# Long convolution, block 0: transform matmuls placed between products, transfers and small products moved, sums in another order

## The chip, the cores and the metric

One Trainium2 chip, one core. The metric is the device time of one execution in microseconds (us). The engines are PE (matmuls; PEld is its weight load), DVE (vector), ACT (scalar, activations), POOL (GpSimd) and SP, which here only issues DMAs. Each engine works through its own queue in order. DMAs issued by SP travel on queue q1, DMAs issued by POOL on q0; the same 16 DMA engines serve both.

## The reference, cut to what matters

```python
x = A_u                                     # 1 x 2048 x 576
sa, ca, ga, sb, cb, gb = (silu(c) @ w_mod).reshape(1, 6, 1, 576)   # in order
h = layernorm(x) * (1 + ca) + sa
K = 2 * real(sum_n C[d,n] dt[d] exp(A[d,n] dt[d] l))               # 576 x 2048, N = 128
y = irfft(rfft(h, 4096) * rfft(K, 4096))[:2048] + h * D_skip       # a long convolution
x = x + ga * y
h = layernorm(x) * (1 + cb) + sb
out = x + gb * (relu(h @ w1) @ w2)          # 576 -> 4608 -> 576
```

All in float32. Large matmuls are done with values split in a high and a low part of the type fp32r, so that one product takes several matmuls.

## The kernel before, in words

The 2048 positions are worked in four blocks of 512. The convolution is done block by block with transforms of 1024 points in four parts (`transform`, `butterfly1`, `butterfly2`), and the channels of a block in two halves of 288 (p = 0 and 1). Block 0's convolution, `conv0`, stands alone at the start of the program; those of blocks 1 to 3 are generators that are woven into the feed-forward (`ffn`) of the block before. `KGen` makes the kernel K of the convolution: 576 channels in six groups of 96. For a group, powers W1 (built by `doubling`) and W2 are multiplied on PE in `products`: 192 small matmuls. `first` is a generator that `conv0` calls step by step: group 4's doubling and products, group 5's doubling, group 5's products. `rest`, at the start of the feed-forward, makes the rest of K from W1, W2 and Z, which were stored to DRAM (W1d, W2d, Zd) and are loaded again.

The names that matter below:

- early: both tables of the forward transform (fcu, fck), loaded early into a buffer that frees later. fcU, fcK: the same tables in their lasting place. gc: the table of the inverse. fcKn, gcn: negated parts of these.
- ZU, ZK: transforms of h and of K for the first half; U0, K0, Y0, V0: their spectra, the product, and the inverse's first step. Z1, WK, U1, K1, Y1, V1: the same for the second half. `transform1` makes WK by two matmuls for each part, so that no butterfly's first step is needed.
- kd, kt: K's rows, stored to DRAM (`store`) and loaded in another layout (`load_kt`). `src_K` adds the skip weight dsk to kt's first row.
- Ud, Rd: spectra of halves, stored by POOL (`save`).
- sb, cb, gb: products of the conditioning vector with 576x576 pieces of w_mod (`mod_late`), through one buffer wm, one after the other: load on POOL's queue, 25 matmuls, ACT copies, two transposes.
- `back`: the inverse's matmuls ps_i, DVE's addition to x2 (the residual stream) and its statistics st. `norm2`: square roots on ACT, h2, transposes ps_t, and xh, xl, xs for the feed-forward.
- r1, r2 (both r in the profile): pieces of w1 and w2 from DRAM, two buffers each; `split1` and `split2` make the high part w on ACT and the low part on DVE, and the low part is stored (L1d, L2d). hps: the first matmul of the feed-forward; hh, hl: its split result, hh by ACT, hl by DVE, in two PSUM buffers; acc: the second matmul.

The order on each engine is set in three ways. In `conv0` most DVE operations and SP DMAs go through `kept` while `self.pinned` is true, which ties each to the one before it on its engine; what isn't tied is put in order by a scheduler at build time. SP's DMAs use eight semaphores in turn, so a DMA waits until the one eight places ahead has landed.

Of the kernel before, what the change touches and what calls it, by code (L numbers as in the profile page):

```python
# [18 lines left out]
P = 128  # L19
# [27 lines left out]
class KGen:  # L47
# [165 lines left out]
    def doubling(self, g):  # L213
# [4 lines left out]
        for i, m in enumerate((1, 2, 4, 8)):  # L218
            X, out = W1[:, :, 0:m].rearrange(flat), W1[:, :, m : 2 * m]
            zr, zi = (  # L220
                Z[:, r, i].rearrange("p (u c) -> p u c", u=2).unsqueeze(2).broadcast_to([P, 2, 2 * m, H])
                for r in range(2)
            )
            for u in (slice(0, 1), slice(1, 2)) if m > 2 else (slice(0, 2),):
                n = u.stop - u.start
                shape = dict(u=n, a=m, r=2)
                if m == 8:
                    t = self.pt.tile([P, 16 * H], F32, tag="T0", bufs=2, name="T0")
                    T = self.pt.tile([P, 16 * H], F32, tag="T1", bufs=2, name="T1")
                else:  # L230
                    t = self.pt.tile([P, 8 * H], F32, tag="t", bufs=2, name="t")[:, : 2 * n * m * H]
                    T = self.ps.tile([P, 512], F32, tag="T", name="T")[:, : 2 * n * m * H]
                t, T = (x.rearrange("p (u a r c) -> p u a r c", **shape) for x in (t, T))
                v(t.rearrange(flat), X[:, u], zr[:, u], op=ALU.mult)
                v(T.rearrange(flat), X[:, u], zi[:, u], op=ALU.mult)
                add = p if m == 8 else v
                add(out[:, u, :, 0], t[:, :, :, 0], T[:, :, :, 1], op=ALU.subtract)
                add(out[:, u, :, 1], t[:, :, :, 1], T[:, :, :, 0], op=ALU.add)

    def products(self, ps, W1, W2, u):  # L240

        for q in range(12):
            for dd in range(4):
                ch = dd * 12 + q
                for r in range(2):
                    self.nc.tensor.matmul(  # L246
                        ps[32 * dd : 32 * dd + 32, 12 * u + q, :],
                        W2[:, r, :, ch],
                        W1[:, u, :, r, ch],
                        start=(r == 0),  # L250
                        stop=(r == 1),
                    )

    def first(self, setup, mod, norm):
# [52 lines left out]

        def multiply(g):
            kps[g] = self.bank(f"kps_{g}")[:, :384].rearrange("p (q a) -> p q a", a=16)
            for u in range(2):  # L310
                self.products(kps[g], self.W1[g], W2s[g][u], u)

# [33 lines left out]
        double(4)  # L346
        multiply(4)
        yield
# [117 lines left out]
class Body:  # L466
# [108 lines left out]
    def mod_weights(self, w, col, eng):  # L575
        v = self.I["w_mod"]
        eng.dma_start(out=w[:, 0:4], in_=v[0:512, col].rearrange("(k p) c -> p k c", p=P))
        eng.dma_start(out=w[:64, 4], in_=v[512:576, col])

    def mod_lhs(self, cb):  # L580
# [6 lines left out]

    def mod_late(self):

# [4 lines left out]
        for i, nm in ((3, "sb"), (4, "cb"), (5, "gb")):  # L594
            w = cv.tile([P, 5, D], F32, tag="wm", bufs=1, name=f"wm_{nm}")
            self.mod_weights(w, slice(i * D, (i + 1) * D), nc.gpsimd)
            yield
# [118 lines left out]

    def transform(self, src, fc, Z):

        nc = self.nc
        for n2 in (0, 2, 1, 3):  # L720
            for c in range(2):
                ps = self.cps.tile([P, 512], F32, tag="cps", bufs=self.nps, name="ps_f")
                o = ps[:, :PC].rearrange("p (a b) -> p a b", a=4)
                nc.tensor.matmul(o, fc[:, n2, c, :], src(n2), start=True, stop=True)  # L724
                nc.scalar.activation(Z[:, n2, c], ps[:, :PC], AF.Copy)  # L725
# [214 lines left out]
    def norm2(self, s, x2, xp, st=None):  # L940
# [15 lines left out]
        for n2 in range(4):  # L956
            if s == 0 and n2 % 2 == 0:
                nc.vector.tensor_scalar(
                    h2[n2][:, :D], x2[:, n2], rs[n2][:, 0:1], rs[n2][:, 3:4],
                    op0=ALU.subtract, op1=ALU.mult,  # L960
                )
                nc.scalar.activation(h2[n2][:, D:], h2[n2][:, 512:D], AF.Copy)
                continue
# [27 lines left out]
    def conv0(self, ctx, c, kg, first, late):  # L991

        nc, I = self.nc, self.I

# [11 lines left out]
        self.pinned = True  # L1006

        def load(t, a):
            self.kept(nc.sync.dma_start(out=t, in_=a))

        def stores():
            for dst, src in self.held:
                load(dst, src)
            self.held.clear()
# [18 lines left out]
        next(first)  # L1033
        run(self.transform(src_K(0), early[:, 1], ZK))
        next(first)
# [31 lines left out]
        self.xp = [self.pool(ctx, "xa", side="right")]  # L1067
        W = S(0, "W")
# [4 lines left out]
        WK = S(1, "WK")  # L1073
        run(self.transform1(src_K(1), self.fcK, fcKn, WK))
        next(mod)
# [31 lines left out]
        root = self.sm.tile([P, 1], F32, name="root")  # L1107
        nc.scalar.activation(root, x2[:, 3, 0:1], AF.Sqrt, scale=0.0, bias=self.eps)
        self.cv = self.pool(c, "cvb")
        next(self.start)  # L1110
        back(1, lambda n2: [(g(n2, c), V1[:, n2, c]) for c in range(2)])
        next(mod, None)
        run(self.norm2(0, x2, self.xp[0], st))
        self.pinned = False
        self.half_tag = "T"

    def load_kt(self, s, p):
# [6 lines left out]
        if s == 0:  # L1124
            self.kept(d)
        return kt
# [267 lines left out]
```

## Time and profile before

| | us |
|---|---|
| three runs | 1411.89 (median), 1408.91, 1412.83 |
| the profiled execution | 1413.05 |
| its span, first to last instruction | 1411.3 |

The profile is of one execution. A row of the timeline gives start, duration, engine, line, operation, output<-input, shapes and count, and in brackets the idle time before it and what ended that. A row of DMA issues gives the KB of one and the median time from issue to landing. The feed-forward begins at 241.82 us. Ahead of it come K's first part and block 0's convolution; only these and the feed-forward's first weights are touched by the change. The changed program has other line numbers: those of the profile of before are used here.

### The profile page before, as it was taken

Reading aid. Unit: us, or ns where it says so; the run is one execution under the profiler, and the core shown is the slowest. Engines: PE = TensorE matmul, PEld = TensorE weight load, DVE = VectorE, ACT = ScalarE, POOL = GpSimd, SP = SyncE. Lnnn points to the kernel's source line nnn. Section 1 sums busy time; section 2 is a strip of 40 time slices with the busy share of each in tenths; the row PEclk is TensorE's granted clock in tenths of the full one; section 3 lists DMA queues with packets and bytes.
Section 4 is the critical chain, followed back from the end, with each engine's and each line's share of the span. In section 5 each row is a group of like instructions: output and inputs, shape, how many; then the busy total and the mean of one; then the engine's idle time right before and its main releaser. Section 6 shows DMA issues by size and latency. Waiting matters only on the chain. (4 is left out here: it accounts for less than half of the span.)

```text
span 1411.3 us, 25953 instructions
## 1 busy us (share of the span) xinstructions
PE 1243.7 (88%) x10600; PEld 984.0 (70%) x10600; DVE 881.8 (62%) x1353; ACT 502.7 (36%) x1008; POOL 197.8 (14%) x271
## 2 busy tenths in 40 slices
PE   6023677999999988799999989999999999999997
PEld 3023455778777776577777867777887888888885
DVE  4987968999875796658744986263999232010111
ACT  6975224222223412432233224434322253233331
POOL 1776311011111100021011010000010000000000
PEclk9555688999999999899999999999999999999998
DMA  6665777689887947489678995665988657666661
GB/s 189 226 245 197 282 262 285 222 290 328 277 292 242 322 155 296 159 318 374 223 249 309 330 368 167 194 227 175 386 313 316 200 156 212 201 191 199 196 187 57
DMA packets 135510, 346.36 MB, mean 245 GB/s; under 512 B 23456, under 2 KB 23744, under 8 KB 135392
## 3 DMA queue, kind: packets, MB, share of 16 engines
q1 hardware_dynamic: 108112, 221.57, 48.2%
q0 software_dynamic: 26992, 122.55, 23.6%
q8 instruction: 83, 1.36, 0.4%
q10 hardware_dynamic: 288, 0.59, 0.1%
q14 instruction: 35, 0.29, 0.1%
HBM read 263.26 MB, written 81.40 MB: 244 GB/s over the span
## 5 line engine op out<-in xcount | busy, mean ns | idle before, releaser
L1204 PE MATMUL acc<-hh,w 128*128 128x512 f32 x1296 | 429.2, 404 | 6.0 <-DVE w L488 6.0
L1179 PE MATMUL hps<-xh,w 128*128 128x512 f32 x1152 | 398.1, 406 | 0.0
L1185 DVE SCALAR_TENSOR_TENSOR hl<-hps,hh 128x512 fp32r<-128x512 f32 x144 | 99.1, 688 | 323.6 <-ACT hh L1184 323.3
L1204 PEld LDWEIGHTS acc<-hh,w 128*128 128x128 f32 x1296 | 244.5, 190 | 59.8 <-DVE w L488 7.6
L1204 PE MATMUL acc<-hl,w 128*128 128x512 f32 x720 | 280.5, 399 | 0.0
L1179 PEld LDWEIGHTS hps<-xh,w 128*128 128x128 f32 x1152 | 219.3, 191 | 48.2 <-ACT xh L982 0.6
L1179 PE MATMUL hps<-xl,w 128*128 128x512 f32 x576 | 230.0, 399 | 0.2 <-DVE xl L987 0.2
L1184 ACT ACTIVATE hh<-hps 128x512 fp32r<-128x512 f32 x144 | 86.0, 598 | 338.8 <-PE hps L1179 336.1
L1163 ACT ACTIVATE w<-r 128x576 fp32r<-128x576 f32 x144 | 98.7, 686 | 259.6 <-PE acc L1204 217.3
L1204 PEld LDWEIGHTS acc<-hl,w 128*128 128x128 f32 x720 | 136.1, 189 | 28.5
L1179 PEld LDWEIGHTS hps<-xl,w 128*128 128x128 f32 x576 | 110.3, 191 | 24.8 <-DVE xl L987 1.3
L246 PE MATMUL kps<-W,W 128*32 128x16 f32 x2304 | 39.8, 219 | 92.9 <-POOL W L59 60.0
L1154 ACT ACTIVATE w<-r 128x640 fp32r<-128x640 f32 x144 | 105.5, 733 | 38.5 <-DMA L1d<-w 33.5
L1179 PE MATMUL hps<-xs,w 128*128 128x512 f32 x288 | 103.6, 421 | 11.0 <-ACT w L1154 4.4
L246 PEld LDWEIGHTS kps<-W,W 128*32 128x32 f32 x2304 | 37.6, 151 | 96.0 <-POOL W L59 61.4
L421 PEld LDWEIGHTS kps<-W1r,W2r 128*32 128x32 f32 x3456 | 68.5, 146 | 31.1 <-issue 21.7
L488 DVE TENSOR_TENSOR Y<-Y,T 128x1152 f32<-128x1152 f32 x64 | 85.0, 1351 | 0.2
L421 PE MATMUL kps<-W1r,W2r 128*32 128x48 f32 (+2 forms) x3456 | 77.2, 238 | 7.8 <-issue 4.9
L1312 POOL DMA_DIRECT2D out_dram<-x x16 | 8.8, 550 | 492.4 <-DVE x L1310 492.4
L1179 PEld LDWEIGHTS hps<-xs,w 128*128 128x128 f32 x288 | 54.2, 192 | 24.9 <-DVE w L488 5.3
L488 DVE TENSOR_TENSOR w<-r,w 128x64 fp32r<-128x64 f32 (+2 forms) x108 | 58.3, 572 | 14.3 <-ACT w L1154 12.0
L725 ACT ACTIVATE Z<-ps_f 128x288 f32<-128x288 f32 x104 | 42.2, 409 | 68.6 <-PE ps_f L724 62.5
(192 smaller groups left out, 1414.6 us busy)
## 6 DMA issues: line engine op xcount, KB each, us to landing
r<-in_w_dram SPq DMA_DIRECT2D x144, 320.0 KB, 3.7
r<-in_w_dram SPq DMA_DIRECT2D x144, 288.0 KB, 3.5
w<-L1d SPq DMA_DIRECT2D x108, 320.0 KB, 3.0
w<-L2d SPq DMA_DIRECT2D x108, 288.0 KB, 3.2
W2r<-W2d POOLq DMA_DIRECT2D x18, 1536.0 KB, 10.0
W2d<-W SPq DMA_DIRECT2D x12, 1536.0 KB, 7.7
Ua<-Ud POOLq DMA_DIRECT2D x15, 1152.0 KB, 10.7
W<-W1d POOLq DMA_DIRECT2D x18, 768.0 KB, 10.0
```

Of the source, the lines that this page charges most:

```text
L246: self.nc.tensor.matmul(ps[32 * dd : 32 * dd + 32, 12 * u + q, :], W2[:, r, :, ch], W1[:, u, :, r, ch], start=(r == 0), stop=(r == 1),)
L421: nc.tensor.matmul(ps[32 * dd : 32 * dd + 32, q, :], W2[:, r, :, ch], W1[:, :na, r, ch], start=(r == 0), stop=(r == 1),)
L488: return self.kept(self.nc.vector.tensor_tensor(*args, **kw))
L725: nc.scalar.activation(Z[:, n2, c], ps[:, :PC], AF.Copy)
L1154: nc.scalar.activation(w[:, 0], r, AF.Copy)
L1163: nc.scalar.activation(w[:, 0:D], r, AF.Copy)
L1179: nc.tensor.matmul(ps, a, x, start=(i == 0), stop=(i == 13))
L1184: nc.scalar.activation(hh, ps, AF.Relu)
L1185: nc.vector.scalar_tensor_tensor(hl, ps, 0.0, hh, op0=ALU.max, op1=ALU.subtract)
L1204: nc.tensor.matmul(acc[i], a, x, start=(f == 0 and j in (0, 3, 6, 9, 12)), stop=(f == NF - 1 and j in (2, 5, 8, 11, 13)),)
L1312: nc.gpsimd.dma_start(out=ov[:, n2], in_=x2[:, n2])
```

## The change

It does the following.

1. The last addition of `doubling` for the second half of group 5 goes from POOL to DVE.
2. The eight transform matmuls for ZK are issued in four pairs between the products of group 4 (`products`, `between`), and no longer behind them.
3. SP: the stores of group 5's W2 and Zd, and the load of gc, go from behind the first kt load to behind x2's. fcU and fcK are loaded behind the first r; the second half uses early in their place. The negated tables wait for group 4's last product.
4. `mod_late` begins behind Z1; sb's weights wait until the second kt has landed. sb's product follows WK's matmuls, cb's stands between the two inverses, and gb's behind `norm2`.
5. The skip weight is added to the second kt by POOL, not DVE.
6. The inverse of the first half, with its sums, stands ahead of the second half's last butterflies, not behind them.
7. The feed-forward's memory is opened, and its first weights are asked for, behind WK; their splits come with `norm2`'s steps (`next(self.start)` where it yields -1).

```diff
-                add = p if m == 8 else v
+                add = p if m == 8 and (g < NG - 1 or u.start == 0) else v
...
-    def products(self, ps, W1, W2, u):
+    def products(self, ps, W1, W2, u, between):
         for q in range(12):
+            if q % 6 == 3:
+                for _ in range(2):
+                    next(between, None)
...
-        stores()
-        for t, n in ((self.fcU, "fcu"), (self.fcK, "fck"), (self.gc, "gc")):
-            load(t, I[n])
-        for t, a in zip((fcKn, gcn), I["neg"]):
-            load(t, a)
...
-            self.v(ktv[0:1, 0, :, 0], ktv[0:1, 0, :, 0], dv, op=ALU.add)
+            add = nc.gpsimd.tensor_tensor if p else self.v
+            add(ktv[0:1, 0, :, 0], ktv[0:1, 0, :, 0], dv, op=ALU.add)
...
-        run(self.transform(src_K(0), early[:, 1], ZK))
+        ZKs = self.transform(src_K(0), early[:, 1], ZK, self.kept)
+        first.send(ZKs)
+        run(ZKs)
+        for t, a in zip((fcKn, gcn), I["neg"]):
+            d = load(t, a)
+            behind(d, kg.mm)
...
-        self.cv = self.pool(c, "cvm")
-        mod = self.mod_late()
-        next(mod)
-        self.cv = cva
...
         kt.append(self.load_kt(0, 1))
+        kt1 = self.ktd
+        sK1 = src_K(1)
...
-        run(self.transform(lambda n2: hv[:, n2, :, 1], self.fcU, Z1))
+        run(self.transform(lambda n2: hv[:, n2, :, 1], early[:, 0], Z1))
         x2 = self.x2[0] = self.x2p[0].tile([P, 4, D], F32, tag="x2", bufs=1, name="x2_0")
         load(x2, I["x"][0].rearrange("n m d -> m n d"))
-        stores()
+        load(self.gc, I["gc"])
+        for dst, src in self.held:
+            load(dst, src)
+        self.held.clear()
+        self.cv = self.pool(c, "cvm")
+        mod = self.mod_late(lambda d: behind(d, kt1))
         next(mod)
-        late.close()
-        self.ff = self.pool(ctx, "ff", side="right")
-        next(self.start)
-        self.xp = [self.pool(ctx, "xa", side="right")]
+        self.cv = cva
...
-        run(self.transform1(src_K(1), self.fcK, fcKn, WK))
+        run(self.transform1(sK1, early[:, 1], fcKn, WK))
+        late.close()
+        self.ff = self.pool(ctx, "ff", side="right")
+        next(self.start)
+        self.xp = [self.pool(ctx, "xa", side="right")]
         next(mod)
...
-        W = S(2, "W")
-        run(self.butterfly1(Y, W))
-        V1 = S(1, "V1")
-        run(self.butterfly2(W, V1, 1))
         st = self.sums("st2")
...
         back(0, ops)
...
+        next(mod)
+        W = S(2, "W")
+        run(self.butterfly1(Y, W))
+        V1 = S(1, "V1")
+        run(self.butterfly2(W, V1, 1))
         self.cv = self.pool(c, "cvb")
-        next(self.start)
         back(1, lambda n2: [(g(n2, c), V1[:, n2, c]) for c in range(2)])
+        for w in self.norm2(0, x2, self.xp[0], st):
+            if w == -1:
+                next(self.start)
         next(mod, None)
-        run(self.norm2(0, x2, self.xp[0], st))
+        for t, n in ((self.fcU, "fcu"), (self.fcK, "fck")):
+            load(t, I[n])
```

`behind(d, op)` makes the DMA d wait until op has finished; `kg.mm` is the last product of group 4.

How the order moves, at three places. On SP, from the second load of kt to the first r, in the program before:

```order
L1120 DMA kt<-kd_1_58 128x16x72
L1009 DMA x_0_2543<-in_x_dram 128x4x576
L1009 DMA W1d_85<-W_4_1810 128x2x768
L1009 DMA W1d_86<-W_4_1810 128x2x768
L1009 DMA W1d_87<-W_5_1872 128x2x768
L1009 DMA W1d_88<-W_5_1872 128x2x768
L1138 DMA r_2592<-in_w_dram 128x640
```

And in the changed program, SP at the same place:

```order
L1141 DMA kt<-kd_1_58 128x16x72
L1026 DMA x_0_2529<-in_x_dram 128x4x576
L1026 DMA gc<-in_gc_dram 128x1024
L1026 DMA W2d_75<-W_10_1863 128x4x768
L1026 DMA W2d_76<-W_11_1864 128x4x768
L1026 DMA Zd_99<-zs_1910 512x1x48
L1026 DMA Zd_100<-zs_1910 512x1x48
L1026 DMA W1d_85<-W_4_1810 128x2x768
L1026 DMA W1d_86<-W_4_1810 128x2x768
L1026 DMA W1d_87<-W_5_1872 128x2x768
L1026 DMA W1d_88<-W_5_1872 128x2x768
L1159 DMA r_2600<-in_w_dram 128x640
```

gc, two stores of W2 and two of Zd have come between x2's load and the stores of W1; they stood ahead of kt.

On ACT, around the first splits (w<-r) and the square roots of `norm2` (mv), before:

```order
L1154 ACTIVATE w_2751<-r_2592 128x640
L615 ACTIVATE m_cb<-mpt_cb 128x5
L1154 ACTIVATE w_2752<-r_2594 128x640
L1163 ACTIVATE w_2755<-r_2596 128x576
L1108 ACT_TABLE_LOAD
L1108 ACTIVATE root<-x_0_2543,eps 128x1
L780 ACTIVATE mv<-mv,eps 128x1
L609 ACTIVATE row_gb<-mps_gb 128x128
```

And in the changed program, ACT at the same place:

```order
L1121 ACT_TABLE_LOAD
L1121 ACTIVATE root<-x_0_2529,eps 128x1
L625 ACTIVATE m_cb<-mpt_cb 128x5
L1175 ACTIVATE w_2804<-r_2600 128x640
L790 ACTIVATE mv<-mv,eps 128x1
L1175 ACTIVATE w_2805<-r_2602 128x640
L1184 ACTIVATE w_2808<-r_2604 128x576
L790 ACTIVATE mv<-mv,eps 128x1 x2
```

The splits stood ahead of root, which waits for the first half's sums; now they stand behind root and between the square roots.

On PE, from the last transposes of `norm2` to the first hps, in the changed program; before, the four rows of gb stood ahead of all transposes:

```order
L983 MATMUL ps_t<-ident,h_2794 128x128
L983 MATMUL ps_t<-ident,h_2795 128x128
L614 MATMUL mps_gb<-wm_gb,cb 32x128 x20
L614 MATMUL mps_gb<-wm_gb,cb 32x64 x5
L623 MATMUL mpt_gb<-ident,row_gb 128x128
L624 MATMUL mpt_gb<-ident,row_gb 128x32
L1200 MATMUL hps<-xs_2771,w_2804 128x512 x2
```

gb's product and transposes now stand directly ahead of the feed-forward's first matmul.

More of the change, by code (lines that the diff above doesn't have):

```diff
@@ L245, in products @@
                 for r in range(2):
[L246 to L251, printed above, removed]
+                    self.mm = self.kept(
+                        self.nc.tensor.matmul(
+                            ps[32 * dd : 32 * dd + 32, 12 * u + q, :],
+                            W2[:, r, :, ch],
+                            W1[:, u, :, r, ch],
+                            start=(r == 0),
+                            stop=(r == 1),
+                        )
                     )
@@ L306, in double, with multiply @@
                 )
-        def multiply(g):
+        def multiply(g, between=iter(())):
+            self.kept = k.kept if g == NG - 2 else lambda x: x
             kps[g] = self.bank(f"kps_{g}")[:, :384].rearrange("p (q a) -> p q a", a=16)
             for u in range(2):
-                self.products(kps[g], self.W1[g], W2s[g][u], u)
+                self.products(kps[g], self.W1[g], W2s[g][u], u, between)
         def rows(g):
@@ L346, in first @@
         double(4)
-        multiply(4)
+        between = yield
+        multiply(4, between)
         yield
@@ L576, in mod_weights @@
         v = self.I["w_mod"]
-        eng.dma_start(out=w[:, 0:4], in_=v[0:512, col].rearrange("(k p) c -> p k c", p=P))
+        d = eng.dma_start(out=w[:, 0:4], in_=v[0:512, col].rearrange("(k p) c -> p k c", p=P))
         eng.dma_start(out=w[:64, 4], in_=v[512:576, col])
+        return d
     def mod_lhs(self, cb):
@@ L586, in mod_product, with mod_late @@
             self.nc.tensor.matmul(ps, cb[:kp, k, :], w[:kp, k], start=(k == 0), stop=(k == 4))
-    def mod_late(self):
+    def mod_late(self, behind):
         nc, act = self.nc, self.nc.scalar.activation
@@ L595, in mod_late @@
             w = cv.tile([P, 5, D], F32, tag="wm", bufs=1, name=f"wm_{nm}")
-            self.mod_weights(w, slice(i * D, (i + 1) * D), nc.gpsimd)
+            d = self.mod_weights(w, slice(i * D, (i + 1) * D), nc.gpsimd)
+            if i == 3:
+                behind(d)
             yield
@@ L715, in save, with transform @@
         self.nc.gpsimd.dma_start(out=strips(dst, 4), in_=t.rearrange("p a b c -> p a (b c)"))
-    def transform(self, src, fc, Z):
+    def transform(self, src, fc, Z, kept=lambda x: x):
         nc = self.nc
@@ L723, in transform @@
                 o = ps[:, :PC].rearrange("p (a b) -> p a b", a=4)
-                nc.tensor.matmul(o, fc[:, n2, c, :], src(n2), start=True, stop=True)
+                kept(nc.tensor.matmul(o, fc[:, n2, c, :], src(n2), start=True, stop=True))
                 nc.scalar.activation(Z[:, n2, c], ps[:, :PC], AF.Copy)
@@ L1006, in conv0, with behind @@
         self.pinned = True
-        def load(t, a):
[L1009 to L1014, printed above, removed]
+        def behind(d, op):
+            tc.add_manual_dep(
+                d.ins, op.ins.name,
+                mybir.DependencyInfo(mybir.DependencyClass.Sync, mybir.DependencyReason.DATA),
+                reason="behind",
+            )
+        def load(t, a):
+            return self.kept(nc.sync.dma_start(out=t, in_=a))
         early = self.early
         kt = [self.load_kt(0, 0)]
-        stores()
-        for t, n in ((self.fcU, "fcu"), (self.fcK, "fck"), (self.gc, "gc")):
-            load(t, I[n])
-        for t, a in zip((fcKn, gcn), I["neg"]):
-            load(t, a)
         hv = self.h.rearrange("m n (dd p q) -> m n dd p q", dd=4, p=2)
```

8 lines of the change are left out of this document (4 added, 4 removed).

## Prediction

> **What bounds the kernel now.** I read the page's slices first, then its groups, then busy time by stretches, then the waits between 190 and 260 us. The chain of waits is of no use here: its listing begins at 913.89 us, long behind the code that is changed.
>
> ```profile
> span 1411.3 us, 25953 instructions
> PE   6023677999999988799999989999999999999997
> L1179 PE MATMUL hps<-xh,w 128*128 128x512 f32 x1152 | 398.1, 406 | 0.0
> 241.82:247.10 5.28, 5.05 (x15) 3.67 (x16) 4.29 (x9) 4.58 (x8) 0.00 (x0) 0.77 1.02 397
> 250.00:260.00 10.00, 10.00 (x46) 7.97 (x45) 10.00 (x11) 3.14 (x5) 0.71 (x1) 1.00 0.53 149
> DVE K L488 <- ACT WK L764: 10.4, 1, 10.4
> ACT w L1154 <- DMA r<-in_w_dram: 3.6, 1, 3.6
> ```
>
> A slice of the PE line is 35.3 us. From the eighth on PE is nearly full: that is the feed-forward part, whose matmuls L1179 wait for nothing. A stretch row gives length, busy time of PE, weight load, DVE, ACT and POOL, then granted clock, DMA share and GB/s: 250 to 260 us is full at clock 1.00. So an edit ahead of 241.82 us, where the feed-forward starts, moves the end by as much as it moves that start, and no more. Ahead of it the long waits are DVE's 10.4 us for the transform WK, and ACT's 3.6 us for r, the first weights. The execution took 1413.05 us, 1.75 more than its span; the median of the three runs is 1411.89, 1.16 below it. Shifts are worked out in this execution and taken off the median.
>
> **The first half: 3.3 us earlier.**
>
> ```profile
> 158.55 2.17 PE L246 MATMUL kps<-W,W 128*32 128x16 f32 x127 [4.11 <-issue]
> 160.31 4.91 POOL L59 TENSOR_TENSOR W<-T,T 128x384 f32<-128x384 f32 x4 [6.09 <-issue]
> 161.74 4.76 DVE L488 TENSOR_TENSOR W<-ZU 128x576 f32<-128x576 f32 x4
> 169.35 0.31 DVE L593 COPY cb<-ct 128x160 f32<-128x160 f32 x1
> 170.75 1.43 DVE L488 TENSOR_TENSOR W<-ZK 128x576 f32<-128x576 f32 x2 [1.09 <-ACT ZK L725]
> 173.26 1.43 DVE L488 TENSOR_TENSOR W<-ZK 128x576 f32<-128x576 f32 x2 [1.08 <-ACT ZK L725]
> 185.52 2.76 DVE L488 TENSOR_TENSOR V<-Y 128x576 f32<-128x576 f32 x4
> 218.87 2.76 DVE L488 TENSOR_TENSOR W<-Y 128x576 f32<-128x576 f32 x4
> ```
>
> Two of POOL's four additions go to DVE. Four DVE additions of 576 cost 2.76 us alone, 0.69 each, so two of 384 cost about 0.9, and up to twice that beside POOL. Beside POOL's 4.91 us the same four took 4.76; with POOL done 2.4 us sooner they should take 2.76, 2.0 less. The copy (0.31) moves into a later wait. The two waits for ZK (2.17) go if ZK is there at 168.5: its matmuls now stand between the fourth group's products, which sit still anyway for 4.11 us at a time. Sum: 2.0 + 0.3 + 2.2 - 1.2 = 3.3; 1.1 if ZK stays late. V0, done at 188.28, is then done at 185.0.
>
> **The second half: 10 us earlier on DVE, if data are there.**
>
> ```profile
> 186.03 0.38 SPq L1120 DMA_DIRECT2D kt<-kd  x1
> 192.30 2.55 PE L604 MATMUL mps_sb<-wm_sb,cb 128*32 128x128 f32 x50
> 197.68 1.30 PE L761 MATMUL ps_f<-kt,fcK 128*128 128x288 f32 x2 [1.89 <-DVE kt L488]
> 197.20:207.95 10.75, 10.28 (x31) 7.69 (x32) 0.38 (x3) 2.88 (x7) 0.79 (x1) 0.72 1.01 405
> 207.95 2.90 DVE L488 TENSOR_TENSOR K<-WK 128x576 f32<-128x576 f32 x6 [10.37 <-ACT WK L764]
> 221.66 2.90 DVE L488 TENSOR_TENSOR V<-W 128x576 f32<-128x576 f32 x6
> 224.48 0.45 DVE L488 TENSOR_TENSOR x<-ps_i,x 128x288 f32<-128x288 f32 x1
> 224.98 6.89 PE L932 MATMUL ps_i<-V,gc 128*128 128x288 f32 x16 [5.50 <-DVE x L488]
> ```
>
> WK no longer waits for U1, for DVE's kt addition or for sb: its matmuls follow Z1's directly, which ended at 192.30 and now end at 189.0. WK took 10.3 us from 197.68 to DVE's start, at a mean clock of 0.72; behind running matmuls I take 1.5 less (bounds: 2.5 less, nothing). K starts at 197.8, 10 us earlier. POOL's kt addition is not in the trace: more than nothing, less than POOL's 1.2 us for 384 columns of all partitions (4.91 / 4); I take 1. kt left SP at 186.03 behind the fifth group's products, which start earlier now; I put it at 180 and landed and added by 186 (an estimate), so 189 covers it. Were it as late as before, WK would lose some 3 us, which the part on the weights swallows.
>
> The added waits: the negated tables stand behind the fourth group's products on SP, ahead of kd and kt, which come later anyway; they are first wanted by WK, over 20 us on. sb's weights stand behind kt on POOL's queue with Ud, wm_cb and Rd behind them; sb's product now follows WK, whose 10 us hide the load. cb's product stands ahead of the second inverse on PE: wm_cb, asked for near 200, takes 10.9 us as before, and the product (gb's equal one takes 2.22, below) is over by 214, one before V's first part is there. Each of these costs nothing; were wm_cb 4 us late, the inverse would be 3 late. fcU and fcK are next read in the feed-forward.
>
> The Trainium skill, TensorE: Matmul & The Clock Gate, What's actually happening, has PE at half clock until it has been busy for about 3.4 us. A mean of 0.72 over 10.75 us is 6 us at half clock, more than that; by the page WK would be 1 us shorter still, which the next part swallows.
>
> K and the product take 10.9 us as before, the first half's sums 3.4, W and V 5.7: V is done at 217.8 and, with some 4.5 us for the inverse that the sums used to hide, the last sum at 222.5, against 233.7. That is where the gain ends.
>
> **The first weights: the gain is eaten.**
>
> ```profile
> 192.40 0.39 SPq L1009 DMA_DIRECT2D x<-in_x_dram  x1
> 214.72 0.74 ACT L1154 ACTIVATE w<-r 128x640 fp32r<-128x640 f32 x1 [3.55 <-DMA r<-in_w_dram]
> 217.72 0.68 ACT L1163 ACTIVATE w<-r 128x576 fp32r<-128x576 f32 x1 [1.51 <-DMA r<-in_w_dram]
> 232.42 0.71 POOL L379 DMA_DIRECT2D W<-W1d  x1 [19.45 <-PE ps_i L932]
> q0 software_dynamic: 468, 2.00, 60.9%
> q1 hardware_dynamic: 469, 1.34, 41.6%
> W2d<-W SPq DMA_DIRECT2D x4, 1536.0 KB, 8.6
> gc<-in_gc_dram SPq DMA_DIRECT2D x1, 512.0 KB, 7.7
> Zd<-zs SPq DMA_DIRECT2D x4, 96.0 KB, 9.7
> W1d<-W SPq DMA_DIRECT2D x4, 768.0 KB, 14.4
> wm_cb<-in_w_mod_dram POOLq DMA_DIRECT2D x1, 1152.0 KB, 10.9
> W2r<-W2d POOLq DMA_DIRECT2D x4, 1536.0 KB, 10.5
> ```
>
> The queue rows are those of 202 to 210 us, both queues full: packet for packet (468 and 469), POOL's q0 moved 2.00 MB and SP's q1 1.34, 0.418 MB/us together. On SP the first r stands behind x (1.18 MB) and four W1d (3.15); now gc (0.52), two W2d (3.15) and two Zd (0.2) stand there too: 8.53 MB with r, not 4.65. x waits for Z1's last matmul, so it leaves at 189.1. POOL moves Ud, wm_cb, Rd and wm_gb meanwhile, 5.0 MB. From 190.8 (1.7 us to the first packet, an estimate that stands in both sums here), (8.53 + 5.0) / 0.418 = 32.4 us: 223.2. The same sum for the old order, 4.65 and POOL's first 2.5 MB from 194.1, gives 211.2, where ACT got r at 214.72; with those 3.5 us on top r comes at 226.7. That is the lower bound. The rest's loads W, Zr and W2r, 4.9 MB on POOL's queue, follow the second inverse (row 232.42), now near 221.5, and from then SP gets two fifths of the link: the last 4.7 us become up to 11.7, r at 233.7. I take 229.
>
> The Trainium skill, DMA: Bandwidth & Descriptors, Specifications, gives a ceiling of 435 GB/s; the rows give 418, and they decide. By the page r would come 1.3 us sooner.
>
> ACT splits both r before it takes the norm's square roots, and DVE's reciprocals and last sums stand behind those: the second r comes 3 us behind the first (214.72, 217.72), 3.7 at two fifths, so 232.7; with 0.68 for the split, two roots and a reciprocal the first h starts at 234.0.
>
> **Norm, gb and the start.**
>
> ```profile
> 227.90 2.28 DVE L488 TENSOR_TENSOR w<-r,w 128x640 fp32r<-128x640 f32 x4
> 231.81 2.22 PE L604 MATMUL mps_gb<-wm_gb,cb 128*32 128x128 f32 x50
> 235.53 0.57 DVE L958 TENSOR_SCALAR h<-x,mv 128x576 f32<-128x576 f32 x1
> 241.82 1.22 PE L1179 MATMUL hps<-xs,w 128*128 128x512 f32 x2 [0.27 <-DVE xs L985]
> 247.09 0.60 ACT L1184 ACTIVATE hh<-hps 128x512 fp32r<-128x512 f32 x1 [0.40 <-PE hps L1179]
> ```
>
> h at 234.0 is 1.5 earlier than 235.53; with r at its bounds 3.8 earlier to 3.2 later. DVE's 2.28 us of splits move into its wait behind h, which hides them. gb's 2.22 us were in an idle stretch and now stand between PE's last transposes and the first hps; with ACT's three copies and one of its xh steps (0.60, as hh's) between product and transposes, the first hps starts some 3.5 us later relative to h, and ACT's new order in the norm costs 0.7 (estimates). But the first group used to take 5.28 us with gaps, and 14 matmuls at 46 per 10 us take 3.0: of the 2.2 between I take 1.7 back, the rest going to a clock that may have dropped. Net 2.5 later (1.1 to 4.2). Last, ACT's hh stands behind the splits of the next two r2, and the second of these is asked for only once DVE's splits, now behind h, free its buffer, behind fcU and fcK (1.05 MB). From 230.7, 3.3 MB on SP and POOL's last 2.7 end at 245; landing and split bring hh to about 248, when 247.09 plus 1.0 would do. I take 1.5 for what PE loses there (0 to 3.5).
>
> Sum: -1.5 + 2.5 + 1.5 = 2.5 us later: 1415.6 for this execution, 1414.4 against the median. Bounds: 2.7 earlier to 10.9 later.
>
> **Rivals.** (1) The early work is worth its price: r comes by 222.5, DVE's sums are the bound, h starts near 225.5, ten earlier; less 2.5 for gb: 7.5 earlier, 1404.4. For it: while POOL's queue is empty SP has the whole link, and how often that is I only estimate. Against it: ACT's 3.6 us wait for r with half the bytes ahead. (2) Slower: the rest's loads win the link while r and r2 are still on it. r at 233.7 puts h 3.2 later, with gb and hh 8 us in all: 1419.9. It decides from r at about 231. For it: equal packet counts with larger packets on POOL. (3) The spread transform doesn't bring ZK early, the fetch pauses staying as they are: 2.2 us more, 1416.6; it goes with the neighbours.
>
> **How the numbers follow.** A measurement of this kernel can tell 0.3%, 4.2 us, from no change. The forecast and its neighbours within that: 0.46. Rival 1: 0.21. Rival 2 with the worse part of 3: 0.33. The range 1405 to 1421 reaches over both rivals' prices.
>
> **What would show it.** Right: WK's wait on DVE under 4 us; the first r at ACT at 226 to 234, behind a DVE that waits for ACT's square root; hps starting 9 to 11 us behind the first h. Wrong: DVE's sums run through without a wait for ACT (rival 1), or PE waits for DVE's w after the second group for more than 4 us (rival 2).

## The result

| | median, us | runs | lowest to highest |
|---|---|---|---|
| before | 1411.08 | 15 | 1403.47 to 1419.48 |
| changed | 1417.10 | 15 | 1410.14 to 1426.12 |

The ratio changed to before is 1.0062, 95% interval 1.0044 to 1.0081; a second set of 12 runs gave 1.0043 (1.0020 to 1.0066). So the change costs 3 to 11 us. The profiled execution took 1415.28 us. Its page, span and slices of PE:

```profile
span 1413.5 us, 25950 instructions
PE   5124772999998988799999989999999999999997
```

The seventh digit, 212 to 247 us, fell from 7 to 2: PE stands still just ahead of the feed-forward. The timeline of the changed kernel from the first half on, columns as before:

```profile
155.72 3.54 DVE L495 TENSOR_TENSOR T<-W,Zp 128x768 f32<-128x768 f32 x4
179.75 2.76 DVE L495 TENSOR_TENSOR V<-Y 128x576 f32<-128x576 f32 x4
194.90 2.90 DVE L495 TENSOR_TENSOR K<-WK 128x576 f32<-128x576 f32 x6 [2.75 <-ACT WK L774]
211.90 2.90 DVE L495 TENSOR_TENSOR V<-W 128x576 f32<-128x576 f32 x6
190.03 12.03 SPq L1026 DMA_DIRECT2D Zd<-zs  x2
202.11 12.09 SPq L1026 DMA_DIRECT2D W1d<-W  x4
214.25 2.25 SPq L1159 DMA_DIRECT2D r<-in_w_dram  x2
217.47 0.73 POOL L386 DMA_DIRECT2D W<-W1d  x1 [4.18 <-PE ps_i L942]
234.85 0.74 ACT L1175 ACTIVATE w<-r 128x640 fp32r<-128x640 f32 x1 [20.92 <-DMA r<-in_w_dram]
235.81 0.16 DVE L795 RECIPROCAL mv<-mv 128x1 f32<-128x1 f32 x1 [19.59 <-ACT mv L790]
240.26 0.68 ACT L1184 ACTIVATE w<-r 128x576 fp32r<-128x576 f32 x1 [2.31 <-DMA r<-in_w_dram]
241.24 0.56 DVE L968 TENSOR_SCALAR h<-x,mv 128x576 f32<-128x576 f32 x1
247.37 2.22 PE L614 MATMUL mps_gb<-wm_gb,cb 128*32 128x128 f32 x50
250.85 0.73 PE L1200 MATMUL hps<-xs,w 128*128 128x512 f32 x2
251.85 1.24 ACT L1184 ACTIVATE w<-r 128x576 fp32r<-128x576 f32 x2
254.35 0.60 ACT L1205 ACTIVATE hh<-hps 128x512 fp32r<-128x512 f32 x1 [1.25 <-PE hps L1200]
```

DVE begins K of the second half 13 us earlier than in the kernel before, and then waits 19.59 us for a square root, which on ACT stands behind the split of the first r; that r is 20 us late. hps begins at 250.85 instead of 241.82, the first hh 7.3 us later. Where the time of the link went, by stretches (length, busy PE, PEld, DVE, ACT, POOL, clock, DMA share, GB/s), first the kernel before, then the changed one:

```profile
150.00:160.00 10.00, 4.09 (x234) 3.88 (x236) 9.79 (x22) 0.00 (x0) 4.13 (x4) 0.60 1.04 382
224.00:236.00 12.00, 9.55 (x68) 6.55 (x68) 10.38 (x32) 2.14 (x10) 3.58 (x6) 0.73 0.53 166
```

```profile
150.00:160.00 10.00, 10.00 (x331) 7.86 (x325) 9.76 (x21) 2.48 (x6) 3.64 (x4) 0.83 0.02 5
224.00:236.00 12.00, 0.00 (x0) 0.00 (x0) 0.19 (x2) 0.92 (x2) 0.00 (x0) 0.50 1.03 407
```

The changed kernel leaves the link empty from 150 to 160 us (5 GB/s) and then has it full from 188 to 236 (367 to 407 GB/s in each 12 us; in the kernel before 201, 416, 303 and 166): the moved stores gave away a stretch in which the link had been full of them, and came back ahead of the first r. The queues from 224 to 236 us (packets, MB, share):

```profile
q0 software_dynamic: 644, 3.27, 67.5%
q1 hardware_dynamic: 645, 1.61, 35.1%
```

POOL's queue, by now the rest's loads, and SP's move equal numbers of packets, but SP gets a third of the bytes.

### The profile page after: what moved, and what is told of

The parts are those of the page before. It is cut to its first block, busy times and chain, and to the rows that moved or that the text cites. A ratio compares the mean times of both kernels' runs of the same rounds, so it can differ in the third digit from the quotient of the medians.

```text
span 1413.5 us, 25950 instructions
## 1 busy us (share of the span) xinstructions
PE 1231.3 (87%) x10600; PEld 978.0 (69%) x10600; DVE 878.8 (62%) x1354; ACT 502.7 (36%) x1008; POOL 195.4 (14%) x270
## 3 DMA queue, kind: packets, MB, share of 16 engines
q8 instruction: 83, 1.36, 0.4%
## 5 line engine op out<-in xcount | busy, mean ns | idle before, releaser
L428 PEld LDWEIGHTS kps<-W1r,W2r 128*32 128x32 f32 x3456 | 68.3, 146 | 28.9 <-issue 18.1
```

The costliest lines, as they stand in the source:

```text
L428: nc.tensor.matmul(ps[32 * dd : 32 * dd + 32, q, :], W2[:, r, :, ch], W1[:, :na, r, ch], start=(r == 0), stop=(r == 1),)
```

## The experiments

All ratios are against runs of the kernel before on the same chip, five rounds each (before_again was only profiled); the other columns are of one profiled execution, in us: the first split of r on ACT, the first h, the first hps, the first hh.

| | first r | h | hps | hh | ratio, 95% |
|---|---|---|---|---|---|
| before | 214.72 | 235.53 | 241.82 | 247.09 | |
| before_again | 212.28 | 233.55 | 239.79 | 245.06 | |
| changed | 234.85 | 241.24 | 250.85 | 254.35 | 1.0062 (1.0044 to 1.0081) |
| after_again | 228.23 | 232.83 | 243.98 | 250.57 | 1.0043 (1.0020 to 1.0066) |
| e1 | 208.87 | 229.84 | 238.72 | 252.61 | 1.0060 (1.0038 to 1.0083) |
| e2 | 229.76 | 233.07 | 242.63 | 254.80 | 1.0077 (1.0049 to 1.0105) |
| e3 | 224.84 | 229.03 | 237.25 | 247.31 | 1.0048 (1.0025 to 1.0070) |
| e4 | 212.14 | 231.28 | 238.01 | 243.29 | 0.9998 (0.9977 to 1.0020) |
| e5 | 216.84 | 225.29 | 232.60 | 237.86 | 0.9986 (0.9961 to 1.0011) |
| e6 | 206.43 | 227.28 | 236.16 | 239.69 | 1.0057 (1.0039 to 1.0075) |
| e7 | 214.32 | 233.59 | 251.68 | 255.21 | 1.0037 (1.0012 to 1.0063) |
| e8 | 205.85 | 223.67 | 230.50 | 235.76 | 0.9970 (0.9949 to 0.9991) |
| e8_again | 208.58 | 227.63 | 234.71 | 239.98 | 0.9962 (0.9936 to 0.9989) |
| e9 | 205.19 | 222.01 | 231.13 | 243.81 | 1.0046 (1.0024 to 1.0068) |

**Two profiles of one kernel.** Nothing is edited.

> The changed kernel once more, unedited, for a second profile of it: is the first r at ACT always near 235, or did that one execution happen to be late? Theory A (the place of the rest's loads against r's bytes decides, and a shift of 2 us ahead of them is enough to turn it, as e3's r at 224.84 against 234.85 suggests): the first r anywhere between 224 and 236, the first hh at 246 to 255, since the third r2 comes no sooner in any of them. Rival (e3's gb product itself brought r forward): r at 233 to 236 again.

> The kernel before once more, for a second profile of it: the first r at ACT at 213 to 217, the first hps at 240 to 244, the first hh at 245 to 249; by how much these differ between two executions says how far a shift of the start between two single profiles can be trusted.

In the second profile of before r and hps came 0.7 and 0.2 us ahead of the stretches expected, hh as expected. The two profiles of before differ by 2.0 us at the first hh, those of the changed kernel by 3.8, and by 6.6 at the first r: one profile gives a start to within some 4 us. Part of this arises ahead of every edit: DVE's last four multiplications T of `doubling` begin at 158.28 and 155.98 in the two profiles of before, at 155.72 and 157.17 in those of the changed kernel. In the second profile of the changed kernel r came at 228.23, and something else held hh:

```profile
243.98 0.73 PE L1200 MATMUL hps<-xs,w 128*128 128x512 f32 x2
249.99 0.68 ACT L1184 ACTIVATE w<-r 128x576 fp32r<-128x576 f32 x1 [4.33 <-DMA r<-in_w_dram]
250.57 0.58 ACT L1205 ACTIVATE hh<-hps 128x512 fp32r<-128x512 f32 x1
```

The group of 14 matmuls takes 3.3 us, so its sum was there at 247.3; hh stood on ACT behind the split of the third r2, which had not landed. In this execution that wall, not the first r by itself, set the start. Theory A holds in all its points; r's place is a matter of a few us ahead of it.

**e1: the stores earlier.**

```diff
         for t, a in zip((fcKn, gcn), I["neg"]):
             d = load(t, a)
             behind(d, kg.mm)
+        load(self.gc, I["gc"])
+        for dst, src in self.held[:4]:
+            load(dst, src)
+        del self.held[:4]
```

and the other held stores behind the second kt.

> The changed kernel, but gc, the two W2d and the two Zd leave SP right behind the negated tables, and the four W1d right behind the second kt, so that only x2 (1.18 MB) stands ahead of the first r after Z1. Theory A (the backlog of transfers behind x2 makes r late, and r sets the start of the feed-forward): ACT gets the first r at 200 to 212 instead of 234.85, DVE's sums run through without a wait for ACT of more than 3 us, the first h is at 221 to 226 instead of 241.24, the first hps 15 to 20 us earlier than 250.85, and the time is 8 to 12 us below the kernel before (ratio 0.991 to 0.994). Rival B (the rest's loads on POOL's queue or something else makes r late): first r at 225 or later, time not below that of before. Rival C (the feed-forward's first block waits for the rest's work anyway and swallows an earlier start): first hps 15 to 20 us earlier, but the time within 0.3% of before.

```profile
171.47 2.15 PE L250 MATMUL kps<-W,W 128*32 128x16 f32 x128 [5.16 <-issue]
178.22 0.43 PE L250 MATMUL kps<-W,W 128*32 128x16 f32 x6 [4.60 <-issue]
208.87 0.74 ACT L1178 ACTIVATE w<-r 128x640 fp32r<-128x640 f32 x1 [2.51 <-issue]
252.02 0.68 ACT L1187 ACTIVATE w<-r 128x576 fp32r<-128x576 f32 x1 [11.62 <-DMA r<-in_w_dram]
254.31 1.43 PE L1203 MATMUL hps<-xs,w 128*128 128x512 f32 x2 [8.95 <-ACT hh L1208]
```

r came 26 us earlier and hps 12, short of the 15 to 20 expected (K of the second half slipped to 201.20: group 5's products paused, kd and kt went out late). Yet the first hh was only 1.7 us earlier, and the time did not move. A's first sentence holds, that the transfers behind x2 make r late; its second, that r sets the start, does not: the third r2 is a second wall, at 252.02, close to the 249.99 above. Neither rival foresaw it.

**e6: e1, with the third r2's split behind the first hh and hl** on ACT and DVE (an order, no wait).

> The kernel of e1 (stores ahead), and beside it the split of the third r2 on ACT and DVE stands behind hh and hl of the first group, not ahead of them. e1's profile had the first hps at 238.72, but hh, which needs only that group's sum (ready near 242), at 252.61, directly behind the third r2's split at 252.02, for whose r ACT had waited 11.6 us. Theory A (the third r2, asked for only when DVE's splits behind h free its buffer, is the second wall, and ACT's order makes hh wait for it): the first hh at 241.5 to 243.5, PE's wait of 8.95 us before the third group gone or cut to under 4, the time 5 to 9 us below e1's, ratio to before 0.999 to 1.003. Rival (the third r1 comes no sooner than the third r2, so that PE stops at the third group anyway): the first hh at 241.5 to 243.5, but PE's wait moves behind it, and the time stays within 2 us of e1's.

```profile
239.69 0.60 ACT L1221 ACTIVATE hh<-hps 128x512 fp32r<-128x512 f32 x1 [1.85 <-PE hps L1216]
248.56 0.69 ACT L1194 ACTIVATE w<-r 128x576 fp32r<-128x576 f32 x1 [6.12 <-DMA r<-in_w_dram]
251.69 3.42 DVE L398 TENSOR_TENSOR W1r<-W,Zr 128x1536 f32<-128x1536 f32 x2
256.77 0.68 DVE L1222 SCALAR_TENSOR_TENSOR hl<-hps,hh 128x512 fp32r<-128x512 f32 x1
257.60 0.76 PE L1216 MATMUL hps<-xs,w 128*128 128x512 f32 x1 [6.60 <-DVE hl L1222]
```

hh left the wall, and the second hh and hl stood behind the same split. On DVE the second hl stood moreover behind 6.7 us of the rest's multiplications (T and W1r, 250.02 to 256.77), so that PE stopped 6.60 us one group later. As the rival said, the time stayed at e1's, though by the third r2 and the rest's work, and not by the third r1. Moving the first hh alone did not cure the late load.

**e2: the rest's first loads wait for the first r2's split**, through `add_manual_dep` on its first DMA.

> The changed kernel, but the first load of the rest on POOL's queue (and with it all behind it) waits until ACT has split the first r2. Theory A (r shares the link packet for packet, and the rest's 4.9 MB take more than half of it from 218 us on): the first r is at ACT at 225 to 228 instead of 234.85, the first hps 7 to 10 us earlier; the time 4 to 8 us below the changed kernel's, less what the later rest costs in the feed-forward. Rival (SP's own queue limits, the other queue takes nothing from it): first r at 233 to 235, time as the changed kernel's or slower.

r at 229.76 lies between the two profiles of the unedited kernel, so what it gained can't be told; the third r2 was split at 254.22, behind the shifted loads. Counted from DVE's last T, r came 72.6 us on, against 79.1 and 71.1 in the two profiles of the changed kernel and 56.4 and 56.3 before: with the rest's loads out of the way some 16 us of r's delay are left, which must come from what was asked for ahead of r. The bytes of the rest only changed places, and the time is not better.

**e3: gb's product ahead of norm2**, one line moved.

> The changed kernel, but gb's product stands ahead of norm2 again, in PE's long wait. Theory A (gb between the last transposes and the first hps lies on the path): first r at 234 to 236 and first h at 240 to 242 as in the changed kernel, the first hps 6.5 to 7.5 us behind the first h instead of 9.6; the time 2 to 3 us below the changed kernel's. Rival (gb's matmuls bring the clock up, and without them the first group runs at half clock): the first hps 2.5 us earlier, but the first hh only 0 to 1.5 us earlier, and the time the same.

hps began 8.2 us behind h, against 9.6 and 11.2 in the two profiles of the changed kernel and 6.3 before: 1.4 to 2.9 us less, about what was expected, though not down to 6.5 to 7.5. The ratio can't be told from the changed kernel's, and the profiled execution, 1408.97 us, was the fastest of e3's ten.

**e4: parts 1 and 2 alone, on the kernel before.**

> The kernel before with parts 1 and 2 of the change alone (the two additions on DVE, ZK's matmuls between group 4's products). Theory A (the first half's gain is real and is passed on, since x2 and with it r leave earlier too): V0 ends 4 to 6 us earlier than 188.28, the first r at ACT 3 to 6 us earlier than 214.72, the first hps 3 to 6 us earlier than 241.82, ratio to before 0.996 to 0.998. Rival (a later wait takes the gain: kt, sb or wm_cb come no earlier): V0 earlier, but K of the second half at 206 to 208 as before, and the time within 0.1%.

V0 ended at 182.16 (179.40 and 2.76), the first hps at 238.01, 1.8 and 3.8 us ahead of the two profiles of before. The ratio, 0.9998, is inconclusive: its interval still has 0.998. Counted from DVE's last T, V0 ended 3.0 to 3.3 us earlier than in the profiles of before, but K of the second half began only 0.7 to 0.9 earlier: kt left SP 31.8 us behind that T, against 27.8 and 28.5. So the rival's later wait took most of the gain. V0's end does show that the spread products bear a full link: the stores went out from 144 to 157 us here, as in the kernel before.

**e5: stores in the half-empty stretch behind the second kt, splits and gb in their old places.**

```diff
+        load(self.gc, I["gc"])
+        for dst, src in self.held[:4]:
+            load(dst, src)
+        del self.held[:4]
...
+        next(self.start)
         back(1, lambda n2: [(g(n2, c), V1[:, n2, c]) for c in range(2)])
-        for w in self.norm2(0, x2, self.xp[0], st):
-            if w == -1:
-                next(self.start)
         next(mod, None)
+        run(self.norm2(0, x2, self.xp[0], st))
```

> The changed kernel with four edits: gc, W2d and Zd leave SP right behind the second kt and ahead of x2 (a stretch in which the link was half idle), fcU and fcK right behind the negated tables; the first splits stand ahead of the second half's last sums again, as in the kernel before, so that the next r1 and r2 are asked for some 20 us sooner; gb's product stands ahead of norm2 again. Theory A (two walls, the first r and the third r2, take the gain of the early second half; with both gone DVE's sums set the start): K of the second half at 194 to 197, the first r at ACT at 210 to 217, the first h at 221 to 225, the first hps 6 to 7.5 us behind it, the first hh at 231 to 237, ratio to before 0.989 to 0.994. Rival B (the stores still keep r back): the first r at 222 or later, ratio above 0.997. Rival C (the feed-forward's first block swallows an earlier start, since its own transfers and the rest's work end later): the first hh at 231 to 237 as with A, but the lead falls to under 4 us within that block, ratio above 0.997.

The places came nearly as A had them (first r 216.84; hh 237.86, 0.9 us behind its stretch), the time did not: no change clear of noise, where 0.989 to 0.994 was expected. The ratio is C's, but C has the lead lost inside the first block, and the profile doesn't show that: the span is 7.7 and 10.7 us shorter than in the two profiles of before, hh 9.2 and 7.2 earlier.

**e9: part 3 undone.** The loop over `held`, fcU, fcK, gc and the negated tables go back to the start of `conv0`; the rest of the change stays.

> The changed kernel with part 3 alone undone: the stores of W2d and Zd, fcU, fcK, gc and the negated tables leave SP at the old place, behind the first kt (in the changed kernel the link moves 7 and 3 GB/s from 150 to 160 us, in the kernel before 403 and 362). Theory A (part 3 is what makes r late; the spread products bear the full link, since e4 had both and V0 ended at 182.2): V0 at 181 to 184, K of the second half at 194 to 197, the first r at ACT at 206 to 211, the first h at 221 to 225, the first hps 9 to 11 us behind it; the third r2, asked for behind h, still holds the first hh back to 238 to 247. Time 0 to 6 us below that of before (ratio 0.996 to 1.000), 6 to 12 below the changed kernel's. Rival (the late third r2 is the whole loss, r costs nothing by itself): first hh at 249 or later, time as the changed kernel's.

```profile
205.19 0.74 ACT L1176 ACTIVATE w<-r 128x640 fp32r<-128x640 f32 x1 [3.72 <-DMA r<-in_w_dram]
231.13 0.73 PE L1201 MATMUL hps<-xs,w 128*128 128x512 f32 x2
227.78 6.31 SPq L1164 DMA_DIRECT2D r<-in_w_dram  x2
243.22 0.68 ACT L1185 ACTIVATE w<-r 128x576 fp32r<-128x576 f32 x1 [10.41 <-DMA r<-in_w_dram]
243.81 0.58 ACT L1206 ACTIVATE hh<-hps 128x512 fp32r<-128x512 f32 x1
```

r is 23 to 30 us earlier than in the changed kernel, hps 13 to 20, hh 7 to 11 (its group was done at 234.4: 9.4 us lost behind the third r2, asked for at 227.78). In the profile A's places for r and hh hold, r 0.8 us ahead of its stretch; the time, 1.0046, is the rival's.

**e8: e9, with the splits and gb in their old places** (the last lines of e5's diff). Of the change this leaves parts 1, 2, 5 and 6, the early table, sb and cb in their new places, and the first weights asked for behind WK; the stores, the splits and gb are back.

> The kernel of e9, and beside it the first splits ahead of the second half's last sums and gb's product ahead of norm2, as in the kernel before: what is left of the change are parts 1, 2, 5, 6, the early table and sb behind WK. Theory A (the first r and the third r2 were the two walls): the first r at ACT at 206 to 211, the third r2 there before the first group's end, the first h at 221 to 224, the first hps 6 to 7.5 us behind it, the first hh at 231 to 236, ratio to before 0.988 to 0.994. Rival C (the feed-forward takes longer when it starts sooner, as e5's time, 0.14% below before with a first hh 9.2 us earlier in its profile, suggests): first hh at 231 to 236, ratio 0.995 to 0.999.

> The kernel of e8 once more, unedited. Its first hh came at 235.76, 11.3 and 9.3 us ahead of the two profiles of before, but its time is only 0.30% (4.2 us) below. Theory A (its profiled execution started sooner than its executions do on average, as the two profiles of the changed kernel differ by 3.8 us at the first hh): the first hh at 238 to 242 this time, ratio 0.995 to 0.998 again. Rival C (the feed-forward gives back about half of an earlier start): the first hh at 234 to 237 again, ratio 0.995 to 0.998. If the first hh is at 234 to 237 and the ratio under 0.994, the shift passes on whole and the first measurement was unlucky.

```profile
205.85 0.74 ACT L1175 ACTIVATE w<-r 128x640 fp32r<-128x640 f32 x1 [3.10 <-DMA r<-in_w_dram]
221.83 14.25 SPq L1163 DMA_DIRECT2D r<-in_w_dram  x2
230.50 1.22 PE L1200 MATMUL hps<-xs,w 128*128 128x512 f32 x2 [0.27 <-DVE xs L995]
234.13 1.24 ACT L1184 ACTIVATE w<-r 128x576 fp32r<-128x576 f32 x2
235.76 0.60 ACT L1205 ACTIVATE hh<-hps 128x512 fp32r<-128x512 f32 x1 [0.39 <-PE hps L1200]
```

The third r2 was asked for at 221.83, 6 us sooner than in e9, and landed in time: hh follows its group. This version beats both kernels, twice: 0.9970 and 0.9962, 4 to 5 us below before. The first ratio is C's and not A's. The second profile has hh at 239.98, as A of e8_again expected: it is likely that the first one had started sooner than this kernel does on average, so its lead of 9.3 to 11.3 us is not to be set against the ratio by itself. From e9 to e8 the ratio falls by 0.8%, 11 us, for nothing but the place of the splits and of gb. In e9's profile the third r2 costs 9.4 us, and hps begins 9.12 us behind h, against 6.83 and 7.08 in e8's two; e3 had moved gb alone without a gain that can be told. So in this company the late splits are most likely the dear part; gb alone was not moved here. Whether undoing them alone, with the stores left late, would help wasn't tried; e5, the nearest, moves the stores too.

**e7: the kernel before, gb behind norm2, its product five times**, to see how far a later start reaches the end.

> The kernel before with gb's product behind norm2 (as in the changed kernel) and issued five times over, so that four of the five only take time. It measures how far a later start of the feed-forward reaches the end. One product takes 2.22 us with the clock up: the first hps should start 6.3 + 3.3 + 4 x 2.22 = 18.5 us behind the first h (17 to 20), 11 to 13 us later than in the kernel before. Theory A (the feed-forward is full, a shift of its start passes on whole): the time 9 to 13 us above before, ratio 1.0065 to 1.0095. Rival C (the feed-forward's first block has slack that takes part of the shift in): the first hps as late, but the time only 3 to 8 us above, ratio under 1.006.

The first hps came 18.1 us behind h, the first hh 8.1 and 10.2 us later than in the two profiles of before; the time rose by 0.37% (0.12 to 0.63), 5.2 us (1.7 to 8.9), which is C's. By the medians half to two thirds arrives, though nearly all of it is not excluded. But the profiled execution was the slowest of e7's twelve: 1422.45 us, 9.4 and 6.3 above the profiled ones of before, where hh had moved by 8.1 and 10.2. In these executions, then, nearly all may have arrived.

## Why the prediction came out as it did

The direction of the forecast, slower, was right; its size, 2.5 us within the measurement's bound, was not. The time that came is rival 2's: 8.0 us, 0.57%, against 0.62% and 0.43% measured; its condition, r from about 231, held in one of the two profiles. That its number fits is in part luck: with the forecast's terms for gb and hh its 3.2 would make 7.2 and not 8, and the second profile reached its late start by another way. Point by point, in the two profiles of the changed kernel:

- **The first half: right.** DVE's last four multiplications T, 3.54 us, began at 158.28; from their end to V0's (188.28) were 26.5 us. Now it is 159.26 to 182.51, 23.3: 3.2 saved where the forecast had 3.3. The rest of V0's 5.8 us lies ahead of the edits; the second profile of before begins T nearly as early, at 155.98.
- **The second half: right.** DVE waits 2.75 us for WK (under 4 expected), K starts at 194.90 (197.8 expected), V is done at 214.80 (217.8). Of the 3 us of difference 1.7 is Z1, which ended at 187.31 and not 189.0, and 1.2 is WK: it took 7.6 us, 2.7 less than before; 1.5 was taken, 2.5 the bound. PE's clock was 1.00 from 188 to 196, against a mean of 0.72 before. In the second profile WK took 8.3 us, at a clock of 0.84. The page TensorE: Matmul & The Clock Gate of the Trainium skill, What's actually happening, had asked for 1 us more than the 1.5: the first trace sides with it, the second lies halfway.
- **The first weights: mechanism right, size off in the first profile.** 229 was taken for r, with 233.7 as the end where the rest's loads win (for which 4.7 us were put between 221.5 and 226.7, where 5.2 lie); it came at 234.85 and 228.23. The 1.7 us to the first packet, in both sums, were 1.05 in the profile of before and 1.94 in the changed kernel's. Two inputs were off. The rest's loads left at 217.47 and not near 221.5, 17 us ahead of r in place of 8; in the second profile they left at 223.60, 5 us ahead of r, and in e3 at 220.50, 4 us ahead. Counted from DVE's last T, r came 79.1 us on with the 17 us, 71.1 and 70.8 with the 5 and 4: whether r's bytes are nearly through before they start decided some 8 us, as rival 2 had it. And SP got 33% of the bytes beside them (1.61 of 4.88 MB), not two fifths: POOL's packets were 5.1 KB against SP's 2.5 here, 4.3 against 2.9 where the two fifths were taken. The Trainium skill, DMA: Bandwidth & Descriptors, Queues, rings and completion order, says that each DMA engine goes round its queues packet by packet; 644 packets against 645 agree with it.
- **From r to h:** 5.0 taken, 6.4 and 4.6 measured. The order on ACT was read rightly: the square roots stand between the splits.
- **gb: right.** hps began 9.6 and 11.2 us behind h (9 to 11 expected, 6.3 before), 3.3 to 4.9 later; the first group then ran its 14 matmuls in 3.3 us in place of 5.28, 2.0 back. Net 1.3 to 2.9, 2.5 taken.
- **hh: the wrong kind of term; this is the step that failed.** It was priced as 1.5 us (0 to 3.5) on top. The third r2 is a wall of its own, since its buffer comes free only with DVE's splits behind h, and its bytes then share the link with the rest's loads. In five profiles (the changed kernel's second, e1, e2, e3, e9) it was asked for 4.7 to 5.8 us behind the first h and split 12 to 17 us after that. Behind a late r it costs nothing (first profile), 3.3 us in the second, about 10 in e1 and 9.4 in e9. That is why an earlier r alone buys nothing in e1 and e9, and why the sum of terms was no good model here: the start is the later of two walls.
- **The sum:** counted from DVE's last T, against the two profiles of before, the second profile has h 1.6 to 1.9 us earlier (1.5 forecast), gb at 2.9 net and hh's wall at 3.3, so hh 4.3 to 4.6 later; the first has h 8.0 to 8.3 later and hh 9.6 to 9.8.
- **The sign given for rival 2** (PE waits over 4 us for DVE's w behind the second group) did not show, though the rival's price did: when r is late enough, the weights behind it have caught up.
- **That a shift of the start passes on whole** was taken for granted, and the runs leave it open. Against the mean of the two profiles of before (246.1), hh moved by 6.4 us in the changed kernel (8.7 and 6.1 measured), 9.1 in e7 (5.2) and -8.2 in the two profiles of e8 (-4.2 and -5.4); counted from DVE's last T, by 7.1, 8.9 and -7.2. The measured times are smaller for e7 and e8, but their intervals reach 8.9 above and 7.2 and 9.0 below. And from the first hh to the end of the profiled execution were 1166.0 and 1171.1 us in the two of before, 1160.9 to 1170.1 in all others but e6's, where hh was moved: the two of before differ by more than what would have to be lost.

Open: e9 is 6.5 us slower than before with a first hh 1.3 to 3.3 us earlier, 1.1 to 1.3 later when counted from DVE's last T. Its profiled execution took 1413.38 us, against 1413.05 and 1416.12 for the two of before; where the rest went, no run separates. e5 starts 7 to 9 us earlier than before and is not faster clear of noise, while e8, whose two starts lie on either side of e5's, is; their intervals overlap. One caution: both profiled executions of before (1413.05 and 1416.12 us) were slower than its median, so shifts between single profiles flatter the other kernel.

## What to carry to other kernels

Before moving transfers out of the way of a wait, look at what the link does in the stretch that they leave and in the one that they enter: here 10 us of the link were left idle, and the load went into the 48 us ahead of the start, which it filled. When an earlier engine meets a load, ask which loads come after it and which release asks for them; the next wall stands there, and removing the first alone showed nothing in the time here (e1, e9). Two walls have to be taken together: e8, which does this, is 0.3 to 0.4% faster than before; for e5, which does it in another way, a gain is not shown.

## What the runs showed of the hardware beside that

- A DMA issue can hold SP when the queue is backed up. The two Zd stores, 96 KB each, took SP 12.03 us to issue in the changed kernel, with 4.85 MB asked for just ahead of them (x, gc and two W2d), and 7.77 in e1; in the kernel before, with the two W2d ahead, 2.10. The four W1d behind them took another 12.09, so the first r was not even issued until 214.25.
- PE's pauses for "issue" among the small products are waits for its instructions, which come over the same DMA engines. The page lists a queue of that kind, 1.36 MB in 83 packets, 16 KB each:

```profile
q8 instruction: 83, 1.36, 0.4%
168.49 2.15 PE L250 MATMUL kps<-W,W 128*32 128x16 f32 x128 [1.60 <-issue]
173.86 0.41 PE L250 MATMUL kps<-W,W 128*32 128x16 f32 x6 [3.23 <-issue]
```

In this profile of the changed kernel two such packets ended at 167.16 and 172.52, 1.3 us ahead of the end of these two pauses. From 105 to 190 us every pause for "issue" of over 0.8 us among the small products ended 1.2 to 1.6 us behind such a packet, in all fourteen profiles. The pauses are longer where the link is full: in e1 5.16 and 4.60 us, with 406 GB/s moving from 170 to 180 us; 1.60 and 3.23 here, with the link about half busy.

- Two executions of one kernel can differ by 6.6 us in the arrival of a load that shares the link (234.85 and 228.23), where their V0 differs by 1.5.
